# Value products in blocks of three, three and two key tiles, the output projection whole behind the loop, and a VectorE row between the halves of a job

## The chip, the core and the metric

The kernel runs on one core of a Trainium2 chip. The core has five engines that run side by side, each through its own list of instructions in order: TensorE (PE, matrix products; its weight loads, PEld, are shown apart), VectorE (DVE), ScalarE (ACT), GpSimd (POOL) and SyncE (SP, which here issues most of the DMAs). They wait for each other by semaphores. The metric is the time of one execution on the device in microseconds (us): the median of three runs, and for all readings one further execution under the hardware profiler.

## The reference

A gated mix of two branches over 2048 tokens of width 512: attention with 32 query heads of width 16 that share one key and one value head, and a SwiGLU feed-forward of inner width 1792. All is float32.

```
g = sigmoid((x * gate_w).sum(-1))
q = x @ wq            # 32 heads of 16;  k = x @ wk, v = x @ wv: one head of 16
p = softmax(q k^T * 16**-0.5)
a = (p v, all heads side by side) @ wo
b = (silu(x @ w_gate) * (x @ w_up)) @ w_down
out = g * a + (1 - g) * b
```

## The kernel before, in words

**Numbers.** Most operands are split into a high and a low part in the format float32r (`split`), and a product is three: high by high, high by low, low by high (`three`). The value products alone use plain float32; the trace shows each of them as two instructions.

**The attention loop.** A unit `u` is one head and one tile of 128 keys, 512 units in all. `score(u, j)` multiplies 128 keys with 1024 queries into one of two score buffers (`pss`, line 637: two products of 64 rows side by side) and has ScalarE take the exponential into the tile `pt` (line 640). A unit has two such scores. `mix(u)` multiplies the values, with a column of ones for the sums, into `po` (line 649: four products of 32 columns each side by side). The loop goes two units at a time (a *block*): the two scores of the next unit, five job steps, a score, three job steps, a score, then `mix` of both units. A head has 16 units, so eight blocks. At a head's end VectorE copies `po` out (654), spreads the sums (656), and takes reciprocals in four pieces (660) and the product (663), one of them per block out of the list `LATER`; the result goes to `o_d` in memory.

**The jobs.** All other products (query projection, gate and up projection, down projection, output projection) are cut into *jobs* of 9 to 15 products that add up in one of three PSUM tiles `pf` (line 178). `Halves` feeds them into the loop a step at a time. A job's products are cut in two halves of 64 contraction rows: it runs first with all its low rows (on one half of the array), then with all its high rows (on the other half), and the high rows of one job run beside the low rows of the next. A step is one product of each. The high rows add to the PSUM tile that the low rows began, so they may begin only when the low ones are done: before, `Halves` waited until two scores that TensorE issues behind them had been passed (`scored`, `sure`). `self.clock` counts steps and scores, and `LONG` for each pair of `mix`; a PSUM tile is taken again `SLACK` counts after the job's last step. A gate job ends in a copy out of PSUM (257), ScalarE's tanh (262, issued ahead of the next `mix` from the list `ACTS`) and a VectorE product (263); the up job that follows ends in three VectorE rows (268, 94, 95).

**The output projection.** Of its four pieces of 128 rows (eight heads each) three were jobs of nine products (`output_part`), fed into the loop when heads 0 to 23 were done; the last piece ran whole at the very end (`finish`, line 104), as 48 products. What is left of the jobs when the loop ends runs whole (128 rows at once, `whole`), twelve jobs with one piece of the last head's normalisation behind each. A small product, `ptop` (718), finds whether scores are so large that a safe path behind the kernel has to run; it doesn't here.

Of the kernel before, what the change touches and what calls it, by code (L numbers as in the profile page):

```python
# [38 lines left out]
KE = KD - 1  # L39
SPOT = 16  # L40
SLACK = 6
LONG = 8
GAP = 36
RATE = 8
FIRST = 5
STOP = 5
# [5 lines left out]
def tile_gated_mix(ctx, tc, x, wq, wk, wv, wo, w_gate, w_up, w_down, gate_w, out):  # L52
# [23 lines left out]
    kmax = cpool.tile([P, 1], F32, name="kmax")  # L76
    top = cpool.tile([P, KD * NCH + 1], F32, name="top")
# [31 lines left out]
    W, WO, HT = {}, [], {}  # L109
# [24 lines left out]
    def load_wo(k):  # L134
        WO.append(load_split(wo[k * P:(k + 1) * P, :], f"wo{k}", 1, ACC[1]))

# [5 lines left out]
    OT, READY = [], set()  # L142


    def allow_o(what):
        READY.add(what)
        if len(READY) == 2:
            load_o(ORDER[0])


    def load_o(c):
        if not OT:
            OT.append(new_x("o"))

        def load(k):
            raw = wp.tile([P, CH], F32, name="wraw", bufs=WRB)
            nc.sync.dma_start(raw, o_d[k * P:(k + 1) * P, c * CH:(c + 1) * CH])
            split(OT[0][0][:, k, :], OT[0][1][:, k, :], raw, nc.gpsimd, nc.gpsimd)
            if k == KE - 1:
                OT[1:] = [c]  # L160

        LOADS.extend([lambda k=k: load(k) for k in range(KE)])

    class Job:
# [4 lines left out]
        def step(self, i, half=None):  # L169
            if i == 0 and not half:  # L170
                self.ps = ps_f.tile([P, CH], F32, name="pf")
                self.terms = self.terms()
            a, b = self.terms[i]
            last = i == self.size - 1
            if half is not None:
                rows = slice(half * RT, (half + 1) * RT)
                a, b = a[rows], b[rows]
            nc.tensor.matmul(self.ps, a, b, start=(i == 0 and not half), stop=(last and half != 0))  # L178
            if last and half != 0:
                self.end(self.ps)  # L180
                for f in self.after:
                    f()
                run(LOADS, 2)
# [118 lines left out]

    def output_part(c, i):
        t = c * TC + i

        def terms():
            r = []
            for k in range(KE):
                r += three([x[:, k] for x in OT[0]], WO[k], (slice(None), slice(i * P, (i + 1) * P)), slice(None))
            return r  # L310

        def add(ps):
            acc = ACC[0]
            nc.vector.scalar_tensor_tensor(acc[:, t, :], ps, g_sb[:, t:t + 1], acc[:, t, :], op0=ALU.mult, op1=ALU.add)

        return Job(3 * KE, lambda: OT[1:] == [c] and len(WO) == KD, terms, add)

# [4 lines left out]
    def jobs():  # L322
        late, parts = [], [[output_part(c, i) for i in range(TC)] for c in ORDER]
        for c, then in zip(ORDER, ORDER[1:]):
            parts[ORDER.index(c)][-1].after.append(lambda then=then: load_o(then))
        early = parts[0] + parts[1] + parts[2]
        count = 0
        for m, c in enumerate(ORDER):
            for fs in GROUPS:
# [4 lines left out]
                if fs[-1] == NF - 1:  # L334
                    if m == NCH - 2:
                        new[-1].after.append(lambda: allow_o("room"))
                    if m < 2:
                        new[-1].after.append(lambda m=m: load_x_again(ORDER[m + 2]))
                if m == NCH - 1 and fs[0] == 0:
                    new[0].after.append(lambda: LOADS.extend([lambda k=k: load_wo(k) for k in range(KD)]))  # L340
                for j, job in enumerate(new):
# [3 lines left out]
                    if m == NCH - 1:  # L345
                        count += 1
                        if count > SPOT and early:
                            yield early.pop(0)
# [3 lines left out]
        yield from early  # L352
        yield from late
        yield from parts[-1]
# [19 lines left out]

    class Halves:
        def __init__(self):
            self.low, self.high, self.wait = None, None, []
            self.done, self.sure, self.scores = 0, 0, []
# [3 lines left out]


        def scored(self):
            self.clock += 1
            self.scores.append(self.done)
            if len(self.scores) > 2:
                self.sure = self.scores[-3]

        def step(self, more):  # L390
# [5 lines left out]
            if not self.high and self.wait and self.wait[0][1] <= self.sure:  # L396
# [3 lines left out]
            self.done += 1  # L400
            self.clock += 1
            if self.low:
# [3 lines left out]
                if not self.low:  # L406
                    self.wait.append((job, self.done))
# [13 lines left out]
    OL = []  # L421

    def load_last(pool):
        OL.extend(pool.tile([P, NCH, CH], F32R, name=n, bufs=1) for n in ("oh", "ol"))
        late = KE * P + P - DH
        for c in ORDER[::-1]:
            raw = pool.tile([P, CH], F32, name="os", bufs=6)
            cs = slice(c * CH, (c + 1) * CH)
            nc.sync.dma_start(raw[:P - DH, :], o_d[KE * P:late, cs])
            nc.sync.dma_start(raw[P - DH:, :], o_d[late:, cs])  # L430
            split(OL[0][:, c, :], OL[1][:, c, :], raw)

    def finish(pool):
        for c in ORDER[::-1]:
            for i in range(TC):
                t = c * TC + i
                ps = ps_f.tile([P, CH], F32, name="pf")
                mm(ps, three([x[:, c] for x in OL], WO[KE], (slice(None), slice(i * P, (i + 1) * P)), slice(None)))
                ot = pool.tile([P, D], F32, name="os", bufs=6)
                nc.vector.scalar_tensor_tensor(ot, ps, g_sb[:, t:t + 1], ACC[0][:, t, :], op0=ALU.mult, op1=ALU.add)  # L440
                nc.sync.dma_start(out[t * P:(t + 1) * P, :], ot)
# [174 lines left out]

    with tc.tile_pool(name="bpool", bufs=2) as bp:
        PT = {}
        PO, LATER = [], []
# [10 lines left out]
        def score(u, j):  # L630
            h, kt = divmod(u, NT)
            if j == 0:
                PT[u] = bp.tile([P, S], F32, name="pt", bufs=PTB)
# [5 lines left out]
            halves.scored()  # L639
            nc.scalar.activation(PT[u][:, j * 2 * CH:(j + 1) * 2 * CH], ps, AF.Exp, scale=SCALE)  # L640

        def mix(u):
            h, kt = divmod(u, NT)
            pt = PT.pop(u)
# [6 lines left out]
            if kt == NT - 1:  # L651

                osb = bp.tile([P, CH], F32, name="osb")
                nc.vector.tensor_copy(osb, po)  # L654
                rsb = bp.tile([P, CH], F32, name="rsb", bufs=1)
# [6 lines left out]
                def store():  # L662
# [4 lines left out]
                    if h == KE * HG - 1:  # L667
                        allow_o("heads")
# [10 lines left out]
        with tc.manual_schedule():  # L679
            score(0, 0)  # L680
            score(0, 1)
            for n in range(NU // 2):
                quota = int((n + 1) * RATE) - int(n * RATE)

                def feed(k):
                    for _ in range(k):
                        if JOBS and n < NU // 2 - STOP or halves.busy():
                            halves.step(n < NU // 2 - STOP)

                u = 2 * n  # L690
                score(u + 1, 0)
                score(u + 1, 1)
                feed(FIRST)
                if u + 2 < NU:
                    score(u + 2, 0)
                    feed(quota - FIRST)
                    score(u + 2, 1)
                run(ACTS, len(ACTS))
                mix(u)
                mix(u + 1)  # L700
                halves.clock += LONG
                if LATER:
                    LATER.pop(0)()
                if n % (NT // 2) == 1 and 0 < u // NT < H - 1:
                    load_head(u // NT + 1)
            assert not halves.busy()

            for _ in range(12):
                assert JOBS[0].ready()
                whole(JOBS.pop(0))  # L710
# [99 lines left out]
```

## Time and profile before

| what | us |
|---|---|
| median of 3 runs (1388.85 to 1390.69) | 1389.07 |
| the profiled execution | 1389.39 |
| its span, from the first to the last instruction | 1387.6 |
| VectorE busy | 525.5 |
| ScalarE busy | 1013.8 |
| GpSimd busy | 388.2 |
| granted TensorE clock, share of full speed | 0.999 |

How to read what the prediction quotes. In the *chain that ended last*, in order of time, a row is the start in us, the length in us and what ran, `xN` being N instructions in a row; the chain is followed back from the last instruction, at each step to what released it. In a *timeline* of one engine a row has the line of the kernel, the operation, what it writes and reads, and in brackets the idle time before it and what ended that. In the *waits* a row has who waited for whom: us in total, times, longest. "issue" is time in which the engine waited for nothing that the profile shows. TensorE instructions overlap, and their ends are modelled, so starts are the better measure. In the loop one step of two halves counts as two instructions, a score as two, a value tile as eight.

### The profile page before, as it was taken

The numbers are of one execution on the slowest core, as the hardware profiler recorded it, in microseconds if no ns is written. First come the engines' busy times: TensorE is split into PE (matmuls) and PEld (weight loads), VectorE is DVE, ScalarE is ACT, GpSimd is POOL, SyncE is SP. The second block draws the span as 40 slices with busy tenths as digits, with TensorE's granted clock in tenths as the row PEclk, the third lists the DMA queues.
The fourth block names the chain that finished last, engine by engine and source line by source line (L and its number), as shares of the span: only waits on it lengthen the run. The fifth ranks groups of instructions, "written<-read, shape, count | busy, mean of one in ns | idle before, by whom it ended". The sixth has DMA issues, their size and how long they took to land.

```text
span 1387.6 us, 25617 instructions
## 1 busy us (share of the span) xinstructions
PE 1372.2 (99%) x10671; PEld 741.8 (53%) x10671; DVE 525.5 (38%) x733; ACT 1013.8 (73%) x1109; POOL 388.2 (28%) x404
## 2 busy tenths in 40 slices
PE   8999999999999999999999999999999999999998
PEld 6655555555555555555555555555555555555586
DVE  5465333243333243233243343333333243332446
ACT  4577787788777788787777787778778788777500
POOL 5140321232131241142131141142144241143152
PEclk9999999999999999999999999999999999999999
DMA  8455210121133131121132131121123231121044
GB/s 268 146 167 197 68 54 24 58 72 41 27 103 81 59 98 32 43 73 46 36 123 61 58 95 35 43 69 51 50 60 101 62 91 36 43 63 51 19 112 159
DMA packets 101258, 106.66 MB, mean 77 GB/s; under 512 B 10000, under 2 KB 69392, under 8 KB 99600
## 3 DMA queue, kind: packets, MB, share of 16 engines
q1 hardware_dynamic: 99552, 104.89, 26.3%
q8 instruction: 86, 1.41, 0.4%
q10 hardware_dynamic: 1584, 0.07, 0.1%
q14 instruction: 36, 0.29, 0.1%
HBM read 75.04 MB, written 29.36 MB: 75 GB/s over the span
## 4 chain that ended last, share of the span: by engine, by line
PE 98%; issue 1%; ACT 0%; DVE 0%; DMA 0%; ACTq 0%
PE pf L178 39%; PE po L649 34%; PE pss L637 22%; PE pf L104 2%; PE pss L530 1%; ACT pt L640 0%; DMA wkv_f<-in_gate_w_dram 0%; PE pss L569 0%; DVE xl L533 0%; DVE rsb L660 0%; DVE rsb L656 0%; DVE os L440 0%; DVE osb L654 0%; DVE hs L257 0%; ACTq L489 0%
## 5 line engine op out<-in xcount | busy, mean ns | idle before, releaser
L640 ACT ACTIVATE pt<-pss 128x1024 f32<-128x1024 f32 x1024 | 966.2, 1031 | 270.5 <-PE pss L637 262.9
L649 PE MATMUL po<-pt,vaug 128*32 128x512 f32 x4096 | 493.5, 598 | 0.0
L637 PE MATMUL pss<-qs,ks 64*128 64x512 f32 x2048 | 414.3, 434 | 3.0 <-ACT pt L640 2.8
L637 PEld LDWEIGHTS pss<-qs,ks 64*128 64x128 f32 x2048 | 174.1, 184 | 313.0 <-ACT pt L640 258.4
L649 PEld LDWEIGHTS po<-pt,vaug 128*32 128x32 f32 x4096 | 106.9, 109 | 222.5 <-issue 219.3
L178 PE MATMUL pf<-xl,wgh 64*128 64x512 f32 (+1 forms) x436 | 166.5, 391 | 0.0
L178 PE MATMUL pf<-xh,wuh 64*128 64x512 f32 (+1 forms) x436 | 164.1, 392 | 0.7 <-DVE hs L257 0.7
L178 PE MATMUL pf<-xh,wul 64*128 64x512 f32 (+1 forms) x436 | 164.2, 391 | 0.0
L178 PE MATMUL pf<-xh,wgh 64*128 64x512 f32 (+1 forms) x436 | 162.1, 390 | 0.0
L178 PE MATMUL pf<-xh,wgl 64*128 64x512 f32 (+1 forms) x436 | 161.4, 391 | 0.0
L178 PE MATMUL pf<-xl,wuh 64*128 64x512 f32 (+1 forms) x436 | 160.1, 391 | 0.0
L178 PE MATMUL pf<-wdh,hh 64*128 64x512 f32 (+1 forms) x417 | 150.5, 390 | 0.0
L94 POOL CAST wuh<-wraw 128x512 fp32r<-128x512 f32 x56 | 34.9, 623 | 413.2 <-PE pf L178 375.1
L178 PE MATMUL pf<-wdl,hh 64*128 64x512 f32 (+1 forms) x417 | 150.1, 390 | 0.0
L178 PE MATMUL pf<-wdh,hl 64*128 64x512 f32 (+1 forms) x417 | 149.2, 390 | 0.0
L94 POOL CAST wgh<-wraw 128x512 fp32r<-128x512 f32 x56 | 34.3, 612 | 388.8 <-PE pf L178 265.0
L660 DVE RECIPROCAL rsb<-rsb 128x128 f32<-128x128 f32 x128 | 116.7, 933 | 1.1
L257 DVE COPY hs<-pf 128x512 f32<-128x512 f32 x56 | 38.6, 689 | 199.2 <-PE pf L178 199.1
L268 DVE TENSOR_TENSOR ht<-ht,pf 128x512 f32<-128x512 f32 x56 | 38.0, 678 | 198.9 <-PE pf L178 198.9
L263 DVE SCALAR_TENSOR_TENSOR ht<-ht,hs 128x512 f32<-128x512 f32 x56 | 44.3, 791 | 111.7 <-ACT ht L262 111.7
L178 PEld LDWEIGHTS pf<-xh,wgh 64*128 64x128 f32 (+1 forms) x436 | 80.4, 184 | 8.8
L178 PEld LDWEIGHTS pf<-xl,wgh 64*128 64x128 f32 (+1 forms) x436 | 80.4, 184 | 8.2
(148 smaller groups left out, 1572.8 us busy)
## 6 DMA issues: line engine op xcount, KB each, us to landing
wraw<-in_B_w_gate_dram SPq DMA_DIRECT2D x56, 256.0 KB
wraw<-in_B_w_up_dram SPq DMA_DIRECT2D x56, 256.0 KB
wraw<-in_B_w_down_dram SPq DMA_DIRECT2D x56, 256.0 KB
qs<-q_d SPq DMA_DIRECT2D x62, 192.0 KB
q_d<-hl SPq DMA_DIRECT2D x16, 256.0 KB
q_d<-hh SPq DMA_DIRECT2D x16, 256.0 KB
o_d<-osb SPq DMA_DIRECT2D x128, 32.0 KB
a_d<-acc SPq DMA_DIRECT2D x4, 1024.0 KB
```

What stands on the lines that cost most here:

```text
L94: eng_hi.tensor_copy(hi, src)
L104: nc.tensor.matmul(ps, a, b, start=(i == 0), stop=(i == n - 1))
L178: nc.tensor.matmul(self.ps, a, b, start=(i == 0 and not half), stop=(last and half != 0))
L257: nc.vector.tensor_copy(g, ps)
L263: nc.vector.scalar_tensor_tensor(t[0], t[0], 1.0, g, op0=ALU.add, op1=ALU.mult)
L268: nc.vector.tensor_tensor(t[0], t[0], ps, ALU.mult)
L530: nc.tensor.transpose(ptv[:, k, j * P:(j + 1) * P], xt[:, i + j, k * P:(k + 1) * P], ident)
L637: nc.tensor.matmul(ps[:, b * CH:(b + 1) * CH], ks[rows, kt * P:(kt + 1) * P], QS[h][rows, j, :], start=True, stop=True)
L640: nc.scalar.activation(PT[u][:, j * 2 * CH:(j + 1) * 2 * CH], ps, AF.Exp, scale=SCALE)
L649: nc.tensor.matmul(po[c * 2 * DH:(c + 1) * 2 * DH, :], vaug[:, kt, :], pt[:, c * CH:(c + 1) * CH], start=(kt == 0), stop=(kt == NT - 1))
L660: nc.vector.reciprocal(rsb[:, w], rsb[:, w])
```

## The change

Five things are changed together.

1. **Blocks.** From the third head on (when the accumulator's pool, and with it room for a fourth tile of exponentials, is open) the blocks of a head have 3, 3, 2, 3, 3, 2 units, with 13, 12 and 8 job steps. The first two heads keep blocks of two with eight steps. In a block, the scores are set apart by `FIRST` = 5 steps, then `NEXT` = 3, and what is left of the quota before the last one.
2. **High rows.** When a job's low rows are issued, VectorE writes one element (`sign`) behind them, and the first high product waits for it. `Halves` starts the high rows `LAG` = 6 counts after the low ones at the earliest.
3. **Output projection.** No part of it is a job any more. Behind the loop all of it runs whole, twelve products for each tile of 128 tokens (192 products). Its inputs are loaded chunk by chunk.
4. **End of the loop.** Steps end ten units before the end; five jobs are left and run whole. The last head's normalisation is issued in two pieces, behind the first and the second of them.
5. **Pools.** The tiles of exponentials have a name each; the tiles of the normalisation come from an outer pool; the load of a next head's queries is issued at a head's first block.

```diff
-RATE = 8
 FIRST = 5
-STOP = 5
+NEXT = 3
+STOP = 10
+EARLY = 24
+BLOCKS = ((3, 13), (3, 12), (2, 8)) * 2
+SMALL = ((2, 8),) * 8
...
-            nc.tensor.matmul(self.ps, a, b, start=(i == 0 and not half), stop=(last and half != 0))
+            ins = nc.tensor.matmul(self.ps, a, b, start=(i == 0 and not half), stop=(last and half != 0))
+            if half == 0:
+                self.lows = ins
+            elif half and i == 0:
+                follow(ins, self.lows)
...
-            if not self.high and self.wait and self.wait[0][1] <= self.sure:
+            if not self.high and self.wait and self.wait[0][1] + LAG <= self.clock:
...
-                    self.wait.append((job, self.done))
+                    self.wait.append((job, self.clock))
+                    tick = nc.vector.memset(sign, 0.0)
+                    follow(tick, job.lows)
+                    job.lows = tick
...
+    def finish(c, pool):
+        for i in range(TC):
+            t = c * TC + i
+            ps = ps_f.tile([P, CH], F32, name="pf")
+            terms = []
+            for k in range(KD):
+                terms += three([x[:, k] for x in OT[c]], WO[k], (slice(None), slice(i * P, (i + 1) * P)), slice(None))
+            mm(ps, terms)
+            ot = pool.tile([P, D], F32, name="ot", bufs=4)
+            nc.vector.scalar_tensor_tensor(ot, ps, g_sb[:, t:t + 1], ACC[0][:, t, :], op0=ALU.mult, op1=ALU.add)
+            nc.sync.dma_start(out[t * P:(t + 1) * P, :], ot)
...
+            while u < NU:
+                if not sizes:
+                    if ACC and not opened:
+                        ROOM.append((ACC[1], f"pt{PTB}"))
+                        opened = True
+                    sizes = list(BLOCKS if opened else SMALL)
+                    if 0 < u // NT < H - 1:
+                        load_head(u // NT + 1)
+                size, quota = sizes.pop(0)
                 score(u + 1, 0)
                 score(u + 1, 1)
-                feed(FIRST)
-                if u + 2 < NU:
-                    score(u + 2, 0)
-                    feed(quota - FIRST)
-                    score(u + 2, 1)
+                later = [(t, j) for t in range(u + 2, u + size + 1) for j in range(2) if t < NU]
+                for i, (t, j) in enumerate(later):
+                    k = quota if i == len(later) - 1 else NEXT if i else FIRST
+                    feed(min(k, quota))
+                    quota -= min(k, quota)
+                    score(t, j)
+                if not later:
+                    feed(FIRST)
                 run(ACTS, len(ACTS))
-                mix(u)
-                mix(u + 1)
-                halves.clock += LONG
+                for t in range(u, u + size):
+                    mix(t)
+                halves.clock += LONG * size
                 if LATER:
                     LATER.pop(0)()
...
-            for _ in range(12):
-                assert JOBS[0].ready()
-                whole(JOBS.pop(0))
-                run(LATER, 1)
-            run(LATER, len(LATER))
...
+        next_job()
+        run(LATER, 3)
+        next_job()
+        run(LATER, len(LATER))
+        load_o(ORDER[0], [KD - 1])
...
+        while JOBS:
+            next_job()
+        load_o(ORDER[1], [KD - 1])
+        for m, c in enumerate(ORDER):
+            finish(c, tp)
+            if m + 2 < NCH:
+                load_o(ORDER[m + 2])
```

What this makes of the engines' lists is shown at three places. TensorE before, in the middle of the loop, the end of a block and the start of the next (`pss` a score, `pf` a job's product, `po` the value products, here two tiles of four):

```order
L637 MATMUL pss<-qs,ks 128x512 x2
L178 MATMUL pf<-wdh,hl 128x512
L178 MATMUL pf<-xl,wgh 128x512
L178 MATMUL pf<-xh,wuh 128x512
L178 MATMUL pf<-xh,wgl 128x512
L178 MATMUL pf<-xl,wuh 128x512
L178 MATMUL pf<-xh,wgh 128x512
L637 MATMUL pss<-qs,ks 128x512 x2
L649 MATMUL po<-pt,vaug 32x512 x8
L637 MATMUL pss<-qs,ks 128x512 x4
```

TensorE in the changed kernel, the end of a block of three with quota 12, from its fifth score on:

```order
L592 MATMUL pss<-qs,ks 128x512 x2
L161 MATMUL pf<-xl,wgh 128x512
L161 MATMUL pf<-xh,wgh 128x512
L592 MATMUL pss<-qs,ks 128x512 x2
L605 MATMUL po<-pt_8482,vaug 32x512 x4
L605 MATMUL po<-pt_8515,vaug 32x512 x4
L605 MATMUL po<-pt_8545,vaug 32x512 x4
L592 MATMUL pss<-qs,ks 128x512 x4
```

Three tiles stand in a row, and before the last score stands one step (two halves) where three stood.

VectorE before, at a head's end (`osb` and `rsb` are the normalisation, `hs` a gate job's copy, `ht` its product):

```order
L654 COPY osb<-po 128x512
L656 STREAM_SHUFFLE rsb<-osb 128x512
L660 RECIPROCAL rsb<-rsb 128x128
L257 COPY hs<-pf 128x512
L263 SCALAR_TENSOR_TENSOR ht<-ht,hs 128x512
```

VectorE in the changed kernel, at a head's end:

```order
L610 COPY osb<-po 128x512
L612 STREAM_SHUFFLE rsb<-osb 128x512
L616 RECIPROCAL rsb<-rsb 128x128
L244 COPY hs<-pf 128x512
L355 MEMSET sign 1x1
L250 SCALAR_TENSOR_TENSOR ht<-ht,hs 128x512
```

The sign stands behind the copy, the shuffle, the reciprocal and, here, a gate job's copy; a job's high rows wait for it.

VectorE behind the loop, in the changed kernel, from the last head's copy to the reduction that `ptop` (line 693 there) needs:

```order
L610 COPY osb<-po 128x512
L612 STREAM_SHUFFLE rsb<-osb 128x512
L255 TENSOR_TENSOR ht<-ht,pf 128x512
L616 RECIPROCAL rsb<-rsb 128x128
L97 CAST hh<-ht 128x512
L98 TENSOR_TENSOR hl<-ht,hh 128x512
L616 RECIPROCAL rsb<-rsb 128x128 x3
L284 SCALAR_TENSOR_TENSOR acc<-pf,c_sb,acc 128x512
L619 TENSOR_TENSOR osb<-osb,rsb 128x512
L691 TENSOR_REDUCE top<-top 128x1
```

TensorE's list there has 17 whole products between the last value product and `ptop`:

```order
L161 MATMUL pf<-wdh,hh 128x512
L161 MATMUL pf<-wdl,hh 128x512
L161 MATMUL pf<-wdh,hl 128x512
L693 MATMUL po<-sel,top 1x8
L161 MATMUL pf<-wdh,hh 128x512
```

The four reciprocals and the product of the last head, which stood between twelve jobs before, now stand between two, ahead of the reduction.

144 lines of the change are left out of this document (45 added, 99 removed).

## The prediction

> **What bounds the kernel now.** The page comes first: how full TensorE is, and what the chain that ended last is made of.
>
> ```profile
> span 1387.6 us, 25617 instructions
> ...
> PE 1372.2 (99%) x10671; PEld 741.8 (53%) x10671; DVE 525.5 (38%) x733; ACT 1013.8 (73%) x1109; POOL 388.2 (28%) x404
> ...
> PE 98%; issue 1%; ACT 0%; DVE 0%; DMA 0%; ACTq 0%
> ```
>
> TensorE is busy 99% of the span and is 98% of the chain. So only TensorE's own time counts, or a wait that it does not have yet. Next comes the chain in order of time: one whole block of the attention loop, then, near its end, one with a job step fewer and the start of one without steps.
>
> ```profile
> 1283.59 0.67 PE pss L637 x4
> 1284.25 1.17 PE pf L178 x10
> 1285.42 0.28 PE pss L637 x2
> 1285.70 0.70 PE pf L178 x4
> 1286.40 0.23 PE pss L637 x2
> 1286.62 1.85 PE po L649 x16
> 1288.48 0.67 PE pss L637 x4
> ...
> 1293.38 0.67 PE pss L637 x4
> 1294.05 1.15 PE pf L178 x5
> 1295.19 0.30 PE pss L637 x2
> 1295.49 0.47 PE pf L178 x2
> 1295.96 0.45 PE pss L637 x2
> 1296.41 1.85 PE po L649 x16
> 1298.27 0.46 PE pss L637 x2
> ...
> 1298.80 1.95 ACT pt L640 x2
> 1300.75 0.04 issue
> 1300.79 0.49 PE pss L637 x2
> 1301.29 1.85 PE po L649 x16
> ```
>
> A block goes from 1283.59 to 1288.48: 4.89 us. In it stand two scores (0.67), five job steps (1.17), a score (0.28), three steps (0.70), a score (0.23) and the value products of two key tiles (1.85). Eight blocks make a head: 39.12 us. The second block has one step fewer, five and two, and still takes 4.89 (1293.38 to 1298.27): its last score takes 0.45 in place of 0.23. What the missing step gave, the score lost again, waiting for a score buffer. **ScalarE stands right behind TensorE.** The third block shows what it waits for: no steps at all, and the chain runs through two exponentials, then 0.04 us, then the last score. There are two score buffers; the fourth score needs the second exponential done, and a sixth would need the fourth.
>
> ```profile
> 1298.80 3.77 ACT L640 ACTIVATE pt<-pss 128x1024 f32<-128x1024 f32 x4 [1.12 <-PE pss L637]
> ```
>
> This row of ScalarE's timeline gives the price: four exponentials in 3.77 us from the first one's start, with ScalarE idle before it. At the head of each block ScalarE starts afresh.
>
> **The change, part by part.** First the blocks: 256 become 196 (16 of two tiles, then six in each of 30 heads). What is a block worth to TensorE alone?
>
> ```profile
> 1301.67 0.13 PEld L649 LDWEIGHTS po<-pt,vaug 128*32 128x32 f32 x4 [0.30 <-issue]
> 1302.10 0.13 PEld L649 LDWEIGHTS po<-pt,vaug 128*32 128x32 f32 x4 [0.30 <-issue]
> ...
> 1306.72 32.07 PE pf L178 x138
> 1338.91 31.06 PE pf L178 x135
> 1369.97 11.21 PE pf L104 x48
> ```
>
> The weight loads of neighbouring value products lie 0.43 us apart, and a key tile has two such rounds: 0.86. The last three rows are full products behind the loop: 273 in 63.13 us, 0.231 each, and a job step of two halves in the loop costs the same (1.17 for five). Eight steps and four scores at 0.231 are 2.77, four rounds 1.72; 4.89 less 4.49 leaves **0.40 us** for going between forms and for the wait at the third score. Sixty blocks fewer would give back 24 us if nothing else ended later. [...]
>
> Now what is late next. A block of three has six scores, and steps between them 5, 3, 3 and then 2 (quota 13) or 1 (quota 12). TensorE alone would begin the value products at 3.03 (1283.59 to 1286.62) plus two scores (0.46) plus five steps (1.16): 4.65 us, or 4.42 with quota 12. The sixth score, however, waits for the fourth exponential. The third block above gives the time for two: from its first score at 1298.27 to the value products at 1301.29, 3.02 us. Four exponentials are 3.77 less 1.95 later: 1.82. So the value products start at **4.84 us**, whichever quota, and TensorE waits 0.19 or 0.42. Three key tiles take 1.85 and 0.86, so a block of three takes 7.55. A head: four times 7.55 and twice 4.89, 39.98 against 39.12. Thirty heads: **+25.8 us**. A saving per block that failed to come would not change this: the wait would shrink instead. [...]
>
> Second, what moves behind the loop. The loop's steps go from 2031 to 2097, by the program's order; the full products behind its last value product go from 321 (the three rows above) to 245, the output projection's 192 among them. Seven more stand between the last blocks, in waits for ScalarE. 76 by 0.231: **-17.6 us**.
>
> Third, the tail's new wait. The flag's one-row matmul (after's L693) now follows 17 full products, 3.93 us, behind the last value product, and needs a VectorE reduction in front of which almost the whole normalisation of the last head stands. Before, that was spread over twelve jobs. Rows of VectorE's timeline for what is in front:
>
> ```profile
> 1306.77 0.69 DVE L654 COPY osb<-po 128x512 f32<-128x512 f32 x1 [10.02 <-PE po L649]
> ...
> 1307.50 0.73 DVE L656 STREAM_SHUFFLE rsb<-osb 128x512 f32<-128x512 f32 x1
> 1308.26 0.95 DVE L660 RECIPROCAL rsb<-rsb 128x128 f32<-128x128 f32 x1
> ...
> 1313.91 0.69 DVE L257 COPY hs<-pf 128x512 f32<-128x512 f32 x1 [1.19 <-PE pf L178]
> ...
> 1317.35 0.75 DVE L297 SCALAR_TENSOR_TENSOR acc<-pf,c_sb,acc 128x512 f32<-128x512 f32 x1 [0.25 <-PE pf L178]
> 1318.01 0.68 DVE L663 TENSOR_TENSOR osb<-osb,rsb 128x512 f32<-128x512 f32 x1
> ...
> 1322.22 0.69 DVE L268 TENSOR_TENSOR ht<-ht,pf 128x512 f32<-128x512 f32 x1 [2.05 <-PE pf L178]
> 1322.94 0.43 DVE L94 CAST hh<-ht 128x512 fp32r<-128x512 f32 x1
> 1323.40 0.69 DVE L95 TENSOR_TENSOR hl<-ht,hh 128x512 fp32r<-128x512 f32 x1
> ...
> 1339.43 0.15 DVE L720 TENSOR_REDUCE fl<-po 1x1 f32<-1x8 f32 x1
> ```
>
> In the new order: gap 0.05, copy 0.69, shuffle 0.73, the up product 0.69, a reciprocal 0.95, cast 0.43, low part 0.69, three reciprocals 2.8, accumulation 0.75, the product 0.68, reduction 0.15: 8.6 us. TensorE stands there after 3.9 and waits **+4.7 us** (bounds: 0, if the chain came early, and 6).
>
> Fourth, VectorE's sign. 164 one-element memsets are added. None is in the trace; the nearest row is the one-element reduction, 0.15. The high half starts at least six counted steps after its low half ended, 1.4 us, and an idle VectorE answers within that: nothing. But at a head's end copy, shuffle and reciprocal hold VectorE for 2.5 us (1306.72 to 1309.21), and the order puts signs, and copies that free a job's PSUM tile, right behind. So answers come 2.8 us into the next block, 3.4 behind one more copy, while high halves that hang on such a sign start 7 to 13 steps in, 2.35 us at the earliest (0.67, 1.17, 0.28 and the sixth step's 0.23).
>
> ```profile
> PE pf L178 <- DVE hs L257: 0.7, 1, 0.7
> ```
>
> Before, TensorE waited so once (this row of its waits). Lower bound 0; upper bound 1 us at each of 30 heads, 30. I take half the heads at 0.6, 9 us, less 0.19 in each of 15 first blocks that the sixth score would have waited anyway: **+6 us**, nearer to the row of before.
>
> At nothing: the fourth tile for exponentials (freed three tiles earlier), the head loads (the same, a head ahead), the stores, now 2.8 us of products apart. The loads of the projection's inputs lie beside 48 products, 11.1 us, each:
>
> ```profile
> 1349.34 0.61 POOL L94 CAST xh<-wraw 128x512 fp32r<-128x512 f32 x1 [5.73 <-PE pf L178]
> ...
> 1351.32 1.09 POOL L94 CAST xh<-wraw 128x512 fp32r<-128x512 f32 x1
> ```
>
> GpSimd needs 1.98 a piece (from one cast to the next), 7.9 for four; without that cover's 3 us for the transfers, the last two chunks would cost 2 us each.
>
> The sum: 25.8 - 17.6 + 4.7 + 6 = +18.9 on the profiled execution's 1389.4: **1408 us**. The median of the runs, 1389.07, lies 0.3 below it, which I leave in the rounding.
>
> **The rivals.** *ScalarE does not hold the sixth score* (faster). If exponentials kept up with TensorE, blocks of three would take 7.36 and 7.13: a head 38.76, 30 heads -10.8; with the tail's -17.6 and +4.7 and the unabsorbed 9 of VectorE, 1375 us. It needs four exponentials and their score in 4.42 us rather than 4.84. Against it: the block with seven steps, no shorter than one with eight. For it: only that TensorE is 98% of the chain.
>
> *VectorE becomes the bound at every head's end* (slower still). If each of 30 heads pays 1 us, less the 0.19, the term is 24 in place of 6: 1426 us. It decides wherever TensorE asks before 2.8 us. For it: the 2.5 us in front. Against it: one such wait before.
>
> *The change moves work and no time is left over.* Without any VectorE wait and without the tail's stall the sum is 1397.6 (1389.4 + 25.8 - 17.6). Were the value products then ready 0.07 us earlier in each of 120 blocks of three, 8.4 us, the time would be 1389. For it: both VectorE terms are my estimates. Against it: all of three terms would have to fall out at once, and ScalarE's 3.77 us leave little to a 0.07.
>
> **How the numbers follow.** Forecast 0.83, its own range 1398 (no VectorE wait and no tail stall: 1389.4 + 25.8 - 17.6) to 1420; the first rival 0.05, the second 0.08, the third 0.04. The range, 1398 to 1422, takes in the forecast's bounds and the lower part of the second rival. A measurement of this kernel tells about 0.2%, 2.8 us, from no change: faster 0.05, same 0.04, slower 0.91.
>
> **What would show it.** Right: blocks of three of equal length, near 7.55, under both quotas; in TensorE's waits a row of scores on ScalarE of some 0.2 and 0.4 us per block; the loop some 26 to 32 us longer, the tail some 13 shorter; one wait of 4 to 5 us at L693. Wrong: blocks near 7.36 and 7.13 (ScalarE term), or waits on signs all over the loop and not only behind a head's end (sign term).

## The result, and the profile after

| | before | after |
|---|---|---|
| median, us (4 runs each, same chip) | 1389.88 (1388.85 to 1391.94) | 1411.55 (1410.92 to 1413.84) |
| profiled execution, us | 1389.39 | 1411.33 |
| its span, us | 1387.6 | 1409.5 |
| granted TensorE clock | 0.999 | 0.996 |

The change makes the kernel slower: ratio 1.0155, 95% interval 1.0137 to 1.0173. The forecast was 1408. First the page of the kernel after: its span, TensorE's share, and the two groups between which a score is passed on (busy time and mean ns, then the idle time before the group and who ended most of it).

```profile
span 1409.5 us, 25925 instructions
...
PE 1378.9 (98%) x10740; PEld 745.2 (53%) x10740; DVE 517.1 (37%) x877; ACT 1008.7 (72%) x1109; POOL 391.1 (28%) x408
...
L595 ACT ACTIVATE pt<-pss 128x1024 f32<-128x1024 f32 x1024 | 961.4, 1037 | 304.2 <-PE pss L592 296.3
L605 PE MATMUL po<-pt,vaug 128*32 128x512 f32 x4096 | 481.1, 597 | 0.0
L592 PE MATMUL pss<-qs,ks 64*128 64x512 f32 x2048 | 428.3, 437 | 11.4 <-ACT pt L595 11.1
```

TensorE still looks 98% busy. That is no proof that it is at its peak, because the ends of its instructions are modelled (in the rows below, two products that begin at 605.08 are given 0.40, and the next begins at 605.32); the starts tell more. A block of three with 12 steps, out of TensorE's timeline of the kernel after (start, length, line; the last row is the next block's first score):

```profile
601.44 0.73 PE L592 MATMUL pss<-qs,ks 64*128 64x512 f32 x4
...
603.14 0.48 PE L592 MATMUL pss<-qs,ks 64*128 64x512 f32 x2
...
604.16 0.40 PE L592 MATMUL pss<-qs,ks 64*128 64x512 f32 x2
...
605.08 0.40 PE L592 MATMUL pss<-qs,ks 64*128 64x512 f32 x2
...
605.32 0.39 PE L161 MATMUL pf<-xl,wgh 64*128 64x512 f32 x1
605.87 0.50 PE L592 MATMUL pss<-qs,ks 64*128 64x512 f32 x2 [0.16 <-ACT pt L595]
606.30 2.78 PE L605 MATMUL po<-pt,vaug 128*32 128x512 f32 x24
609.01 0.73 PE L592 MATMUL pss<-qs,ks 64*128 64x512 f32 x4
```

The block takes 609.01 - 601.44 = 7.57 us, and the value products start 4.86 us into it (forecast 7.55 and 4.84). The sixth score starts 0.55 after the step in front of it, where 0.23 is the pace. The same stretch on ScalarE:

```profile
602.04 5.61 ACT L595 ACTIVATE pt<-pss 128x1024 f32<-128x1024 f32 x6 [1.46 <-PE pss L592]
609.61 3.77 ACT L595 ACTIVATE pt<-pss 128x1024 f32<-128x1024 f32 x4 [1.96 <-PE pss L592]
```

Six exponentials follow each other without a gap, 0.935 us each. ScalarE sets the pace from a block's first score to its last, and is idle 1.96 us under the value products, when there is no score to work on. By the starts of all blocks, the 120 blocks of three have a median of 7.573 us, with 13 steps and with 12 alike; blocks of two are as before (4.90).

The waits of TensorE, as they are named (us in total, times, longest):

```profile
PE pss L592 <- ACT pt L595: 11.1, 60, 1.0
...
PE po L693 <- DVE top L691: 3.3, 1, 3.3
PE pf L161 <- DVE sign L355: 1.6, 4, 0.6
```

And the stretch behind the loop, which begins at 1337.44 us, in windows (start and end, length, then busy us and instructions of TensorE, its weight loads, VectorE, ScalarE and GpSimd, then the granted clock, the DMA share and GB/s):

```profile
1338.00:1342.00 4.00, 3.79 (x16) 2.55 (x14) 3.92 (x8) 0.00 (x0) 3.10 (x4) 1.00 0.48 131
1342.00:1346.00 4.00, 0.68 (x4) 0.37 (x4) 3.62 (x7) 0.00 (x0) 2.75 (x4) 0.87 0.26 74
1346.00:1352.00 6.00, 6.00 (x15) 4.68 (x16) 1.02 (x4) 0.00 (x0) 4.44 (x6) 0.52 0.39 104
1352.00:1378.00 26.00, 26.00 (x117) 21.49 (x116) 6.79 (x10) 0.00 (x0) 8.69 (x9) 1.00 0.40 130
```

TensorE stands still in the second window, which is the flag's wait. In the third it is busy all the time, and yet 15 products take 6 us, 0.4 us each in place of the 0.22 (26 us by 117) of the fourth: the granted clock is 0.52 there.

From the first block's end to the last's, the loop takes 1281.02 us (1250.57 before): +30.45. From there to the end of the span it is 72.02 (80.97 before): -8.95. The loop also begins 0.35 later. So the whole loss is made in the loop, and the tail gives back less than was forecast (-12.9).

### The profile page after: what moved, and what is told of

Its sections match the earlier page's. It is cut to its first block, busy times and chain, and to the rows that moved or that the text cites. A ratio compares the mean times of both kernels' runs of the same rounds, so it can differ in the third digit from the quotient of the medians.

```text
span 1409.5 us, 25925 instructions
## 1 busy us (share of the span) xinstructions
PE 1378.9 (98%) x10740; PEld 745.2 (53%) x10740; DVE 517.1 (37%) x877; ACT 1008.7 (72%) x1109; POOL 391.1 (28%) x408
## 5 line engine op out<-in xcount | busy, mean ns | idle before, releaser
L605 PE MATMUL po<-pt,vaug 128*32 128x512 f32 x4096 | 481.1, 597 | 0.0
L592 PE MATMUL pss<-qs,ks 64*128 64x512 f32 x2048 | 428.3, 437 | 11.4 <-ACT pt L595 11.1
L161 PE MATMUL pf<-xh,wgh 64*128 64x512 f32 x448 | 167.1, 390 | 0.2 <-DVE sign L355 0.2
L161 PE MATMUL pf<-xh,wgl 64*128 64x512 f32 x448 | 166.6, 390 | 0.0
L161 PE MATMUL pf<-xl,wgh 64*128 64x512 f32 x448 | 165.2, 389 | 0.0
L161 PE MATMUL pf<-wdh,hh 64*128 64x512 f32 (+1 forms) x432 | 159.1, 394 | 0.9 <-DVE ht L255 0.8
L161 PE MATMUL pf<-wdh,hl 64*128 64x512 f32 (+1 forms) x432 | 159.2, 392 | 0.2 <-DVE hl L98 0.2
L161 PEld LDWEIGHTS pf<-xh,wuh 64*128 64x128 f32 (+1 forms) x444 | 81.9, 185 | 9.6 <-POOL wgh L97 1.5
L161 PEld LDWEIGHTS pf<-xh,wgh 64*128 64x128 f32 x448 | 82.5, 184 | 8.0 <-issue 0.6
L161 PEld LDWEIGHTS pf<-xl,wuh 64*128 64x128 f32 (+1 forms) x444 | 81.8, 184 | 8.8 <-issue 1.1
```

Source lines behind the costliest of these rows:

```text
L161: ins = nc.tensor.matmul(self.ps, a, b, start=(i == 0 and not half), stop=(last and half != 0))
L592: nc.tensor.matmul(ps[:, b * CH:(b + 1) * CH], ks[rows, kt * P:(kt + 1) * P], QS[h][rows, j, :], start=True, stop=True)
L605: nc.tensor.matmul(po[c * 2 * DH:(c + 1) * 2 * DH, :], vaug[:, kt, :], pt[:, c * CH:(c + 1) * CH], start=(kt == 0), stop=(kt == NT - 1))
```

## The experiments

Ratios below are to the kernel before, run on the same chip in the same batch, with 95% intervals. A difference in us to the kernel after goes across batches, in which the kernel before itself had medians from 1389.4 to 1391.4; where some 2 us matter, block lengths and starts in the traces decide.

**1. Does ScalarE hold the blocks of three?** The second half of each key tile's scores is made as before, but its exponential covers 64 of 1024 columns, and the value products read the first half twice. The same is done to the kernel before.

```diff
-            nc.scalar.activation(PT[u][0][:, j * 2 * CH:(j + 1) * 2 * CH], ps, AF.Exp, scale=SCALE)
+            n = CH // 8 if j else 2 * CH
+            nc.scalar.activation(PT[u][0][:, j * 2 * CH:j * 2 * CH + n], ps[:, :n], AF.Exp, scale=SCALE)
...
-                nc.tensor.matmul(po[c * 2 * DH:(c + 1) * 2 * DH, :], vaug[:, kt, :], pt[:, c * CH:(c + 1) * CH],
+                nc.tensor.matmul(po[c * 2 * DH:(c + 1) * 2 * DH, :], vaug[:, kt, :], pt[:, c % 2 * CH:(c % 2 + 1) * CH],
```

> The changed kernel with half of ScalarE's work left out: of a key tile's two score halves only the first is exponentiated whole, of the second 64 of 1024 columns, and the value products read the first half twice. All scores, value products, steps and waits stay. Theory: ScalarE then no longer holds the sixth score; blocks of three take TensorE's own 7.36 (13 steps) and 7.13 (12 steps) in place of 7.57 both, which is 60 x 0.21 + 60 x 0.44 = 39 us, less 2 to 4 us of VectorE waits that the score waits now absorb: 1373 to 1378, and below the kernel before with the same work left out. Rival (blocks of three are 7.57 because of something on TensorE, such as three tiles of value products in a row): blocks stay at 7.5, time within 5 us of 1411.

> The kernel before with the same half of ScalarE's work left out (of the second score half 64 of 1024 columns are exponentiated, the value products read the first half twice). Theory: TensorE's own work bounds blocks of two, so they stay near 4.89 and the time near 1389, at most 5 us less; then the change, without ScalarE's pace, would be a gain of 11 to 16 us. Rival (ScalarE also paces blocks of two): blocks fall by 0.2 us or more, 50 us less.

The kernel after goes to 1372.43 us (1371.11 to 1373.51; ratio 0.9874, 0.9857 to 0.9890), 39 us less. The one before goes to 1385.72 (1384.40 to 1386.97; 0.9968, 0.9955 to 0.9981), 4 us less. Blocks of three now take 7.38 with 13 steps and 7.14 with 12, while TensorE alone was put at 7.36 and 7.13 in the prediction's first rival. TensorE's waits in the kernel after, so cut, keep one on ScalarE:

```profile
PE pss L592 <- ACT pt L596: 1.0, 1, 1.0
```

This shows both halves of the argument. Larger blocks do save TensorE's time: a head with 66 steps now takes 2 x (7.38 + 7.14) + 2 x 4.89 = 38.8 us, while eight blocks of two with 64 steps take 39.1. And ScalarE's pace is what takes that away. (The 13 us between these two kernels hold the rest of the change too, the tail above all.) The kernel before, so cut, also bears out the prediction's reading of its block with seven steps: that block, 4.89 us before, takes 4.67 now, while blocks with eight steps stay at 4.89.

**2. Would blocks of two with the same steps have been better?**

```diff
-BLOCKS = ((3, 13), (3, 12), (2, 8)) * 2
+BLOCKS = ((2, 8), (2, 8), (2, 8), (2, 9)) * 2
```

> The changed kernel with its blocks undone: eight blocks of two key tiles a head from the third head on, with 8, 8, 8 and 9 steps in turn, so that a head keeps its 66 steps. Sign, whole projection and tail as changed. Theory (ScalarE holds the sixth score of a block of three): a head falls from 4 x 7.57 + 2 x 4.92 = 40.1 us to 8 x 4.89 + 2 x 0.23 = 39.6, so the time falls by about 15 us, to 1394 to 1399. Rival (the larger blocks are a gain of 0.40 us for each of 60 blocks, and the loss lies in the sign or in the projection behind the loop): about 24 us more than the changed kernel, 1435.

1398.91 us (1396.48 to 1400.84), ratio 1.0064 (1.0045 to 1.0082): 12.6 less than with blocks of three, and the rest of the change is still in it. A block with nine steps, from its first score to the next block's, in TensorE's timeline of this kernel:

```profile
602.89 0.74 PE L592 MATMUL pss<-qs,ks 64*128 64x512 f32 x4
...
608.09 0.73 PE L592 MATMUL pss<-qs,ks 64*128 64x512 f32 x4
```

It takes 5.20; the median of such blocks is 5.18. One step more than eight costs some 0.2 to 0.3 there, and experiment 1 showed that one step fewer gains nothing as long as ScalarE has its full work. So a block of two with eight steps is where TensorE and ScalarE are level.

**3. What do the signs do?** The kernel after with the rule of before for the high rows; and the kernel before with the signs alone.

```diff
-            if not self.high and self.wait and self.wait[0][1] + LAG <= self.clock:
+            if not self.high and self.wait and self.wait[0][1] <= self.sure:
...
-                    self.wait.append((job, self.clock))
-                    tick = nc.vector.memset(sign, 0.0)
-                    follow(tick, job.lows)
-                    job.lows = tick
+                    self.wait.append((job, self.done))
```

> The changed kernel without VectorE's sign: the high rows start, as before the change, when two scores have been passed behind the low rows. Blocks, projection and tail as changed. By the program's order this leaves 136 steps with one half only (59 with the sign), and 38 whole products more behind the loop. Theory (blocks of three are held by ScalarE at 7.57 whether their steps are full or not; signs cost TensorE some 2 to 3 us in all): 38 x 0.23 = +8.7, signs -2 to -3: 1416 to 1419. Rival (the sign is what makes the changed kernel slow): 1400 or less.

> The kernel before with the sign alone: a VectorE element behind each job's low rows, for which the high rows wait, at the earliest six counts later. Nothing else is changed. By the program's order 44 steps have one half only (72 before), and 9 whole products fewer stand behind the loop. Theory: -2 us for the products, 0 to 5 us of waits where VectorE is busy at a head's end: 1387 to 1393, no difference that can be told. Rival (each of some 160 signs costs a tenth of a us or more): 1405 or more.

Without signs the kernel after takes 1418.85 us (1418.34 to 1419.01; 1.0196, 1.0172 to 1.0219), 7.3 more. Its loop is 1279.8 long, only 1.2 shorter, with blocks of three at 7.575; but 38 more products stand behind it, because high rows may start later and steps run with one half alone (136 of them, against 59). In the kernel before, the signs make no difference that can be measured: 1390.34 (1388.31 to 1393.18; 0.9998, 0.9986 to 1.0010). So the signs cost about 1 us in the loop, and with these quotas the rule of before costs more than they do.

**4. The tail's wait.** The reduction for which the flag's matmul waits is moved ahead of the last head's normalisation.

```diff
+        nc.vector.tensor_reduce(top[:, KD * NCH:], top[:, :KD * NCH], axis=AX.X, op=ALU.max)
         next_job()
         run(LATER, 3)
...
-        nc.vector.tensor_reduce(top[:, KD * NCH:], top[:, :KD * NCH], axis=AX.X, op=ALU.max)
```

> The changed kernel with one line moved: the VectorE reduction that the flag's small matmul needs stands ahead of the first whole job behind the loop, not behind the last head's reciprocals. Theory: TensorE's wait at the flag's matmul (3.3 us in the waits, 3.8 us from one start to the next) goes, and with it the 5.7 us behind it in which whole products start 0.427 us apart in place of 0.23: together 6 to 7 us less, 1405. Rival A (the slow products have another cause than the wait): 3.5 us less, 1408, and the 0.427 spacing stays. Rival B (the tail is bound by the loads of the projection's inputs, so the wait only moves): within 1 us of 1411.5.

1409.28 us (1407.53 to 1409.55), ratio 1.0137 (1.0120 to 1.0154): 2.3 less, where the theory said 6.5. The wait at L693 is gone, and another has come 9 us later, as rival B had it, though the time is not within its 1 us: TensorE stands 2.7 us (3.04 from one start to the next) for the last piece of the projection's first input, and the clock falls again, as two windows of this kernel show.

```profile
1351.00:1356.00 5.00, 2.22 (x6) 1.17 (x5) 0.00 (x0) 0.00 (x0) 2.65 (x3) 0.73 0.93 300
1356.00:1360.00 4.00, 4.00 (x11) 3.16 (x10) 0.75 (x1) 0.00 (x0) 1.88 (x2) 0.50 0.22 83
```

SyncE's queue in this kernel (start and length of the issuing) says why:

```profile
1341.31 5.71 SPq L381 DMA_DIRECT2D wraw<-o_d  x3
1347.12 1.78 SPq L621 DMA_DIRECT2D o_d<-osb  x4
1350.01 0.36 SPq L381 DMA_DIRECT2D wraw<-o_d  x1
```

The store of the last head's result was ready at 1343.8, but stood behind three loads for the next chunk, which themselves wait for buffers; and the load that TensorE needs reads what this store writes. The second edit puts those three loads behind it:

```diff
-            if len(JOBS) == TC:
-                load_o(ORDER[1], range(KD - 1))
...
         load_o(ORDER[0], [KD - 1])
+        load_o(ORDER[1], range(KD - 1))
```

> The kernel with the early flag reduction (e2), and besides the loads of the second chunk of projection inputs issued behind those of the last head's piece, not ahead of its store. Theory: in e2 SyncE's queue held the last head's store back for 3.4 us behind three loads that waited for their buffer (store issued at 1347.12, product ready at 1343.80); without that the first chunk's last piece is ready 3 us earlier, TensorE no longer stands still, and its products keep 0.23 us: 5 to 6 us less than e2, 1403 to 1405. Rival (the way from the last head's product over memory to the split is too long whatever the order): within 1.5 us of e2's 1409.3.

1405.04 us (1404.22 to 1407.52), ratio 1.0099 (1.0081 to 1.0118): 6.5 less than the kernel after. The granted clock from 1338 to 1378 is 1.00 now. The 6.5 us are what the table below gives for the flag's wait (3.6) and the slow products behind it (2.9).

**5. A version in which the pieces fit.** As long as ScalarE holds it, a block of three takes 7.57 us with 12 steps and with 13, and a 14th step would bring TensorE's own time from 7.38 to 7.61. So: the kernel before with the signs, its output projection still fed in as jobs, and in 20 of the heads blocks of three, three and two with 14, 14 and 8 steps (blocks of two in the others). Besides, the last piece of `wo` and the last head's inputs go to other tiles, and waiting loads are issued ahead of each whole job behind the loop.

```diff
+BLOCKS = ((3, 14), (3, 14), (2, 8)) * 2
+SMALL = ((2, 8),) * 8
+LASTH = 22
...
+                    sizes = list(BLOCKS if opened and u < LASTH * NT else SMALL)
...
+                later = [(t, j) for t in range(u + 2, u + size + 1) for j in range(2) if t < NU]
+                for i, (t, j) in enumerate(later):
+                    k = quota if i == len(later) - 1 else NEXT if i else FIRST
+                    feed(min(k, quota))
+                    quota -= min(k, quota)
+                    score(t, j)
```

> A kernel made of the one before, with the sign, the output projection's jobs still in the loop, and blocks of 3, 3, 2 key tiles with 14, 14 and 8 steps in heads 2 to 21 only, blocks of two with eight steps in all others. 14 steps fill the time in which a block of three waits for ScalarE: TensorE's own 4.65 + 0.23 + 2.72 = 7.60 against 7.57. Theory: a head of 72 steps takes 4 x 7.61 + 2 x 4.9 = 40.2 us, 20 heads cost +22 us, 159 whole products fewer stand behind the loop, -36.6, VectorE waits +3 to +6: about 1379 (1374 to 1385), faster than both kernels. Rival (blocks of three never pay on this chip, each step more costs as much in the loop as behind it): 1389 or more.

1384.76 us (1382.36 to 1389.11), ratio 0.9949 (0.9930 to 0.9967): faster than both, but at the upper edge of what was expected. Blocks of three take 7.61, and 162 whole products stand behind the loop in place of 321. The profiled execution, 1389.11 us, is the longest of the six. Its loop is 1272.5 us long, 21.9 more than before, as forecast, but without the 3 to 6 us that were put down for VectorE. Two things are missing. The tail gives back 27.6 in place of 36.6, and the loop's second block begins 4.9 us later than before; the granted clock was 0.50 for 6.8 us ahead of it (last section). TensorE's longest wait in the tail, and what VectorE does at that time (timeline of the same kernel):

```profile
PE pf L187 <- DVE acc L314: 6.8, 1, 6.8
```

```profile
1351.12 0.43 DVE L99 CAST xh<-os 128x512 fp32r<-128x512 f32 x1 [2.82 <-DMA os<-o_d]
1352.21 0.97 DVE L99 CAST xh<-os 128x512 fp32r<-128x512 f32 x1 [0.66 <-DMA os<-o_d]
1354.14 1.06 DVE L99 CAST xh<-os 128x512 fp32r<-128x512 f32 x2 [0.95 <-DMA os<-o_d]
1355.11 2.06 DVE L314 SCALAR_TENSOR_TENSOR acc<-pf,c_sb,acc 128x512 f32<-128x512 f32 x3
```

The accumulations that free TensorE's PSUM tiles stand behind casts that wait for transfers. The next edit gives the casts to GpSimd:

```diff
-            split(OL[0][:, c, :], OL[1][:, c, :], raw)
+            split(OL[0][:, c, :], OL[1][:, c, :], raw, nc.gpsimd, nc.gpsimd)
```

> The 14-step version (1384.76 us) with both parts of the last head's split made by GpSimd instead of one part by VectorE and one by GpSimd. In that version TensorE stood still for 6.8 us behind the loop, waiting for an accumulation of VectorE that stood in VectorE's queue behind the first part of that split, which itself waited for its transfer; after it the products ran for some 4 us at 0.427 us each (about 2.6 us more). Theory A (VectorE's order is the price): the accumulations are no longer held, the wait and the slow stretch go, -9 us: 1375 us (1373 to 1378). Theory B (the transfer itself is late, and the products of the last head's output wait for it wherever the split is): within 2 us of 1384.76.

1383.91 us (1382.78 to 1389.11), ratio 0.9956 (0.9938 to 0.9974): theory A fell. VectorE's wait went, and one of 6.0 us on GpSimd took its place, as its timeline in this kernel shows:

```profile
1346.44 0.61 POOL L99 CAST xh<-os 128x512 fp32r<-128x512 f32 x1 [1.22 <-DMA os<-o_d]
...
1354.07 0.61 POOL L99 CAST xh<-wraw 128x512 fp32r<-128x512 f32 x1
```

Four pieces that TensorE needs only after 1360 are split first; the one that it needs at 1348.7 comes last, in SyncE's queue too. One line turns that round:

```diff
+        run(LOADS, len(LOADS))
         load_last(tp)
```

> The run before, with one line ahead of the last head's loads: the third load of the second chunk's projection input, for which TensorE stood still for 6.0 us, is now issued by SyncE and split by GpSimd ahead of the four splits of the last head (in the run before it stood behind them in both queues: it was issued at 1346.8 us and split at 1354.1 us, while TensorE needed it at 1348.7 us). Theory A (the wait is a matter of the order in those two queues): the input is there by about 1341 us, the 6 us wait and the stretch of products at 0.427 us behind it (some 2 us) go, and nothing takes their place, since the last head's own parts, split from 1346 to 1354 us, are needed only behind 1360 us: -8 us against the run before, 1376 us (1374 to 1379). Theory B (some other input is just as late): within 3 us of 1383.9, with another wait of several us in its place.

1374.91 us (1372.00 to 1378.37), ratio 0.9877 (0.9853 to 0.9901): 16.5 less than before, and some 37 less than the change as it was made. The 6 us wait is gone. TensorE is busy without a pause through the stretch in which it lay, at a full clock:

```profile
1340.00:1349.00 9.00, 9.00 (x41) 7.19 (x40) 5.01 (x10) 0.00 (x0) 5.34 (x6) 1.00 0.47 126
1349.00:1356.00 7.00, 7.00 (x32) 5.56 (x30) 1.14 (x2) 0.00 (x0) 6.62 (x8) 1.00 0.63 233
```

## Why the prediction was right, and where its terms were off

| step | forecast, us | measured, us | from |
|---|---|---|---|
| blocks, 30 heads | +25.8 | +25.6 | 120 x 7.573 and 293.8 for the 60 blocks of two, less 1177.0 before |
| VectorE at head ends | +6 | +3.0 | what eight heads' first blocks take beyond 7.573 |
| other long blocks | 0 | +1.9 | 0.9 in three other blocks of three, and 1.0 in a block of 5.9 us in the second head |
| 76 products fewer behind the loop | -17.6 | -17.6 | 245 in place of 321 |
| flag's wait | +4.7 | +3.6 | 3.82 between two starts, less 0.23 |
| slow products behind it | 0 | +2.9 | 14 intervals from 1345.75 to 1351.85, less 14 x 0.23 |
| late inputs of the projection | 0 | +2.4 | four intervals of 0.62 to 1.02 at 1380 to 1384 and at 1394 |
| waits for the low part of `ht` | 0 | +0.6 | intervals of 0.38, 0.31 and 0.61 ahead of the flag's matmul |
| sum | +18.9 | +22.4 | 21.9 by the spans |

**The mechanism holds.** The sixth score waits for the fourth exponential, the block is 7.57 under both quotas, and the saving per block is swallowed: experiment 1 takes ScalarE out and blocks of three fall to TensorE's own 7.38 and 7.14. The first rival was right about TensorE and wrong about ScalarE; its 1375 is near what experiment 1 measures (1372.4). The second rival (1426) falls: only eight of 30 heads have a first block above 7.65 us. The third fell with the blocks. That the total came within 3.5 us is in part luck: the two waits on VectorE were put 4.1 too high together, and 7.8 us in four other rows of the table had been left out.

**One expected mark did not show.** The prediction wanted waits of scores on ScalarE of some 0.2 and 0.4 us per block. The waits name 60 of them, 11.1 us, while the lengths of experiment 1 make it 0.19 and 0.43 in 60 blocks each, some 37 us. A wait counts from the modelled end of the product before, and 0.39 of modelled length hides most of a pause of 0.32. Block lengths from start to start decide here, not the sum of the waits.

**VectorE's term** was right in place and in price, and twice too large in number. Of the eleven blocks of three above 7.65 us eight are the first of a head (7, 10, 14, 16, 18, 22, 24 and 30, counted from 0), where copy, shuffle and reciprocal hold VectorE. The forecast was 15 heads at 0.6 less 0.19, so 0.41 each; these eight lose 0.38 each in the mean. In heads 14, 16 and 18 TensorE's waits name the sign, in head 10 VectorE's product `ht` behind the same reciprocal. VectorE and then TensorE at head 14, whose first block starts at 613.98:

```profile
614.11 0.69 DVE L610 COPY osb<-po 128x512 f32<-128x512 f32 x1 [3.80 <-PE po L605]
...
614.85 0.74 DVE L612 STREAM_SHUFFLE rsb<-osb 128x512 f32<-128x512 f32 x1
615.62 0.95 DVE L616 RECIPROCAL rsb<-rsb 128x128 f32<-128x128 f32 x1
616.49 0.63 DVE L244 COPY hs<-pf 128x512 f32<-128x512 f32 x1
617.06 0.06 DVE L355 MEMSET sign<- 1x1 f32 x1
```

```profile
617.26 0.46 PE L161 MATMUL pf<-xh,wuh 64*128 64x512 f32 x1 [0.64 <-DVE sign L355]
```

The sign comes 3.1 us into the block, TensorE goes on at 3.28, and the block takes 8.28. Without signs (experiment 3) nine first blocks are above 7.65, by 1.9 us together in place of 3.0, and the pauses that are named there, again 3.3 us in, are for `ht` and `hs`. So the busy VectorE lengthens these blocks, and the sign is one of several rows for which TensorE then waits. The three other long blocks have no pause for VectorE; what waits in them is scores, for exponentials.

**The tail was mis-sized**, -8.95 in place of -12.9. The flag's wait was there, 1.1 smaller than forecast: the rows in front of the reduction ran as listed, but overlapped a little, and TensorE itself came 0.6 later, having waited for the low part of `ht`. VectorE's timeline of the kernel after:

```profile
1341.67 2.56 DVE L616 RECIPROCAL rsb<-rsb 128x128 f32<-128x128 f32 x3
1344.15 0.65 DVE L284 SCALAR_TENSOR_TENSOR acc<-pf,c_sb,acc 128x512 f32<-128x512 f32 x1
1344.72 0.68 DVE L619 TENSOR_TENSOR osb<-osb,rsb 128x512 f32<-128x512 f32 x1
1345.32 0.15 DVE L691 TENSOR_REDUCE top<-top 128x1 f32<-128x16 f32 x1
```

The step that failed is the one that put the loads of the projection's inputs at nothing because they lie beside 48 products (11.1 us). It allowed 7.9 us for GpSimd's four splits and some 3 for the transfers. For the third chunk it takes 13.9 us from the first load's issue to the last split's end: SyncE issues these loads only behind the output stores of the first chunk, and slowly, since there are two buffers that the splits have to free (SyncE's queue, kernel after):

```profile
1360.61 8.45 SPq L394 DMA_DIRECT2D out_dram<-ot  x4
1369.17 8.78 SPq L381 DMA_DIRECT2D wraw<-o_d  x4
```

GpSimd's timeline of the kernel after shows the chunk's fourth piece split from 1381.10 to 1383.06. TensorE's products with its high and its low part start at 1381.77 and 1383.12, 0.94 and 1.02 behind the products ahead of them.

```profile
1381.10 0.61 POOL L97 CAST xh<-wraw 128x512 fp32r<-128x512 f32 x1 [0.33 <-DMA wraw<-o_d]
1381.79 1.27 POOL L98 TENSOR_TENSOR xl<-wraw,xh 128x512 fp32r<-128x512 f32 x1
```

And the price of the flag's wait was taken as its length; the 2.9 us that follow it, at a granted clock of 0.52, were nowhere in the sum.

## What to carry to other kernels

A larger block pays only while every engine that the block passes through has time for it: count the longest chain through the few buffers in between (here two score buffers and 0.935 us an exponential) against the first engine's own work, and fill the block until the two are level, as 14 steps did here. In an in-order queue, a load that waits for a buffer, or a cast that waits for a transfer, must not stand ahead of the piece that is needed next: in experiments 4 and 5 the first repair each time only moved such a wait from VectorE to GpSimd (3.3 us to 2.7, and 6.8 to 6.0, in TensorE's waits), and the next removed it. A busy share of 98% says little where the ends are modelled (0.39 us for products that start 0.23 apart); compare starts.

## What was not expected of the hardware

After TensorE had stood still in the tail, for 3.04 to 7.19 us from one start to the next, it ran at about half speed for some 4 to 6 us more: the granted clock was 0.52 from 1346 to 1352 in the kernel after, 0.50 from 1356 to 1360 in the first kernel of experiment 4, 0.52 from 1356 to 1361 in the 14-step version and 0.55 from 1355 to 1359 in the version with the casts on GpSimd. In the kernel after, 13 products start 0.427 us apart in that stretch (the third window above), in place of 0.23; in the 14-step version, after 7.19 us, the windows show the same:

```profile
1349.00:1356.00 7.00, 0.19 (x2) 0.09 (x1) 3.26 (x6) 0.00 (x0) 4.52 (x4) 0.86 0.59 183
1356.00:1361.00 5.00, 5.00 (x12) 3.92 (x13) 1.17 (x2) 0.00 (x0) 3.41 (x4) 0.52 0.02 5
```

A wait of 3.6 us so costs 6.5 there. The pauses of under 1.1 us in the same tail are followed by products at 0.33 and 0.23 as usual (granted clock 1.00 from 1378 to 1395), and so is one of 2.38 us (from one start to the next) in the kernel before with signs, whose profiled execution has a mean granted clock of 1.000. The shortest of the waits with a slow stretch behind it is the 3.04 us in experiment 4 (granted clock 0.73, then 0.50). What happens behind a wait between 2.38 and 3.04 us, and what ends a slow stretch, the runs do not show.

Nor is the length of the pause all that counts. At the loop's start TensorE makes two short pauses, in the kernels before and after of 1.43 and 0.91 us from one start to the next. In the profiled execution of the 14-step version a slow stretch of 6.8 us follows; that one follows in the last kernel of experiment 5 too is an estimate from its mean granted clock, 0.997 (0.999 before) although it is 1.00 from 1331 to 1370. The 14-step version in windows as above (granted clock third from the end):

```profile
50.00:53.50 3.50, 2.05 (x11) 0.94 (x10) 0.00 (x0) 2.26 (x3) 0.00 (x0) 1.00 0.52 181
53.50:60.30 6.80, 6.80 (x26) 3.60 (x28) 5.82 (x10) 3.56 (x4) 0.00 (x0) 0.50 0.53 203
```

In the version between them, with the casts on GpSimd, TensorE is as busy in the 3.5 us before, and no slow stretch follows; nor does one in the kernels before and after (granted clock 1.00 from 53.50 to 60.30 in both). The version with the casts on GpSimd:

```profile
50.00:53.50 3.50, 2.04 (x12) 1.42 (x11) 0.77 (x2) 3.40 (x4) 0.00 (x0) 1.00 0.52 177
53.50:60.30 6.80, 6.80 (x49) 3.58 (x50) 5.54 (x9) 5.34 (x7) 0.00 (x0) 1.00 0.53 203
```

What decides between the two is not shown here. Half of 6.8 us is the price, an estimate from the granted clock of 0.50; whether the spread between executions of one kernel comes from such stretches is not shown.
